# A gated mix of a state-space layer and linear attention: state space in residues modulo 8 instead of 4, with a new list of steps

## The chip, the cores and the metric

The kernel runs on one core of one Trainium2 chip, in one launch. The metric is device time in microseconds, the median of repeated runs. A core has engines with queues of their own: PE (matrix products into PSUM, whose 8 banks hold 512 fp32 per partition each), DVE (vector), ACT (scalar, activation tables), POOL (GpSimd) and SP, which here only issues transfers.

## The reference

One input x of 2048 x 512 (bf16) goes through two branches, and a gate mixes them by rows. Branch A is a diagonal complex state space of 512 states, scanned over 2048 steps; branch B is linear attention with 32 heads of 16, whose feature map is a softmax of a projection and of its negative.

```python
x = A_x
g = sigmoid((x * gate_w).sum(-1, keepdims=True))
# A
dt = exp(log_dt);  Lam_bar = exp(dt * Lam);  B_bar = ((Lam_bar - 1) / Lam)[:, None] * Bmat
Bu = einsum("bld,pd->blp", x, B_bar)
for t in range(L):                      # L = 2048
    h = Lam_bar * h + Bu[:, t];  hs.append(h)
a = 2 * einsum("blp,dp->bld", hs, Cmat).real + x * Dskip
# B
q, k, v = heads(x @ wqkv)               # 32 heads of 16
phi(u) = concat(softmax(u @ w_phi), softmax(-u @ w_phi))
kv = einsum("bhsf,bhsd->bhfd", phi(k), v);  z = phi(k).sum(s)
b = merge((phi(q) @ kv) / (phi(q) @ z + 1e-6)) @ wo
return g * a + (1 - g) * b
```

## The kernel before

All of x, its transposition and all intermediates stay in SBUF. **The order of work on PE, DVE, ACT and SP is written out by hand**: each piece of work is a generator `st_*`, `ORDER` is a list of tokens, and the loop at L807 advances one generator by one step for each token. `k5@2` is the next step of `st_k(5)` with PSUM bank 2, `:D` puts an eviction or a scaling on DVE instead of ACT. Every engine runs its instructions strictly in that order, and waits where an operand or a bank isn't ready.

Rows of x are loaded by residue (L225, L231): `xT` holds the rows with r = 0 modulo 4 first, then r = 1, 2, 3, so that a stretch of 512 columns is one residue over 512 cells.

- Branch B. `st_W` transposes the k weights on PE (L295), `st_B` makes block diagonals BD from Wc (L342), `st_f` and `st_w` fold w_phi into the k and q weights (L427). `st_k`, `st_v`, `st_q` project 128 rows at a time (L467) and evict through `evac` (L123 on ACT, L125 on DVE). `x*`, `n*`, `e*`, `s*` (capitals for q) are the feature map: maximum and minimum trees (L503), differences (L514, L520), exponentials (L142), sums, logarithms. `st_a` collects the sums over keys and the gate in two banks (L570, L574), `st_Y` masks them. `phT` are transpositions of the q features by DMA (L557).
- Branch A. `P`, `P2`, `P3`, `P4`, `M` make the parameters, `M` on POOL; `st_D` the diagonal matrices `dg`; `st_i` the cosine and sine tables T2c, T2s of the scan's rotation (L440 to L450); `st_l` scales B by Lam_bar, and SP transposes it to LBT. With j a block of 128 states, `st_g(j, dst, ri)` forms the inputs: for dst 0 those of residue 1 (with 0 folded in through LBT), for dst 1 those of residue 3, with 2 folded in and, through two matmuls on `dg`, residue 1's. `st_z` rotates, scans 512 cells by `tensor_tensor_scan` with decay r4 (L638), rotates back and writes H3, the state after residue 3. `st_h` makes H1 from H3 with two scalings on ACT (L407) and three sums. `st_c` and `st_r` prepare C and C times Lam_bar, `st_K` the direct matrix K0T.
- Output. `st_y(n)` multiplies 128 rows of states by C (L720, L721) and adds K0T or Dskip (L727, L729); `st_o` divides the attention (L740, L744, L747, L753); `st_O` transposes two of its tiles by DMA to oT (L761); `st_t` adds oT times Wo into st_y's bank (L769) and scales by the gate (L777, L779); `st_R` stores.

The start is fixed by these lines: Wk in one load and the three parameter vectors ahead of Wc on ACT's queue.

```python
nc.scalar.dma_start(out=wk_nat, in_=B_wqkv[:, D:2 * D].rearrange("(k p) n -> p k n", p=P))
for n, src in enumerate((A_Lambda_im, A_Lambda_re, A_log_dt)):
    nc.scalar.dma_start(out=vec_n[4 * n:4 * n + 4, :], in_=src.rearrange("(j p) -> j p", p=P))
nc.scalar.dma_start(out=Wc[:], in_=B_w_phi.rearrange("(k hl) e f -> (hl e) k f", hl=8))
```

Of the kernel before, what the change touches and what calls it, by code (L numbers as in the profile page):

```python
# [34 lines left out]
N0 q11@4 a2 s3 q11 c1 c1 a2 a2 v9@7 e4 s3 a2 q4@4 q4 q5@1 z1 g301@0 c1 c0 X0 N0 e4 q6 q5 X1 N1 s3 z1 z1 z1 Lc g301 X1
g301 g300@4 z0 z0 v11@5 g300 q9 z1 e4 s4 v14@6 g300 g311@0 E0 g311 v14 z1 g311 z0 N1 g310@6 g310 z0 g310 s4 z1 s4
g200@4 v8@1 X1 c3 c3 c3 z1 v9 g311 g201@0 E0 N1 g310 g200 E0 E0 v11 v8 s4 q14@6 z3 g200 g210@7 z3 g201 v15@1 h0 h0
q15@4 s4 S0 h0 v13@5 g201 S0 s4 z3 q14 h0 q15 g210 g210 h0 N1 z3 c2 g211@4 g211 v15 X1 g211 c2 v10@6 z3 z3 v13 c2 S0
r1 c3 r0 g210 S0 S0 s3 v12@5 c2 z3 g211 q13@1 z3 S0 s3 z3 z3 v10 v12 z2 q10@0 y0@4 a3 r1 S0 S0 z2 q13 q12@5 a3 a3 a3
K2@1 q10 h3 h3 h3 q12 K0@0 z2 z2 z2 h3 h3 z2 K2 Lo K3@1 y3@5 r0 K1@6 s4 a4 z2 z2 a4 s4 z2 K0 y1@0 a4 z2 y0 X1 N1 a4 Y  # L40
h1 h1 y3 Y Y Y G K3 S0 y3 K1 h1 h2 r1 y0 h2 h2 h1 h1 h2 h2 END S0 o0@6 r1 E1 E1 o0 o0 y1 S0 o1@2 o1 y1 o0 E1 o1 G G
y4@1 E1 y4 S1 y4 o1 y7@6 S1 G S1 N2 o2@2 r3 r3 o2 o2 S1 S1 o2 y7 r0 y7 S1 y6@7 X2 y6 S1 O0 S1 N2 o3@2 o3 o3 X2 N2 X2
o3 y6 r0 X2 t0 N2 t1 t0 X2 y2@4 N2 t1 X3 y2 r2 r2 S1 y5@0 y5 y5 S1 X3 N3 X3 N3 X3 E2 o4@2 O1 o4 E2 o4 o4 y2 t2 r3 r3
t3 t2 o5@2 N3 t3 y9@4 o5 r2 r2 N3 S1 o5 o5 y13@5 E2 y13 o6@2 y9 E2 o6 X3 y9 N3 R1 o6 E3 o6 o7@2 S2 S2 O2 E3 o7 y13 o7
# [21 lines left out]
def kernel(  # L66
# [60 lines left out]
    NOSYNC = mybir.DependencyInfo(mybir.DependencyClass.NoSync, mybir.DependencyReason.DATA)  # L127
    act_st = {"pre": None, "sins": [], "exps": []}

    def order_after(ins, earlier, why):  # L130
        tc.add_manual_dep(ins.ins, earlier.ins.name, NOSYNC, reason=why)

    def pin_act_set():
        pre = nc.scalar.preload_act_table_set(ACT_SET)
        for s_ in act_st["sins"]:
            order_after(pre, s_, "table set after trig")
        act_st["pre"] = pre
        act_st["sins"] = []
        act_st["exps"] = []

    def aexp(**kw):
        ins = nc.scalar.activation(**kw)  # L142
        order_after(ins, act_st["pre"], "Exp/Ln after table-set preload")
        act_st["exps"].append(ins)
        return ins

    def asin(**kw):
        ins = nc.scalar.activation(func=ACT.Sin, **kw)
        order_after(ins, act_st["pre"], "Sin after preload")
        if not act_st["sins"]:  # L150
            for e_ in act_st["exps"]:
                order_after(ins, e_, "trig batch after the preceding Exp/Ln batch")
        else:
            order_after(ins, act_st["sins"][0], "inside one trig batch")
        act_st["sins"].append(ins)
        return ins

    man_g = tc.manual_schedule(engines={mybir.EngineType.PE, mybir.EngineType.DVE, mybir.EngineType.Activation, mybir.EngineType.SP})
# [10 lines left out]
    nc.scalar.dma_start(out=wk_nat, in_=B_wqkv[:, D:2 * D].rearrange("(k p) n -> p k n", p=P))  # L169
    for n, src in enumerate((A_Lambda_im, A_Lambda_re, A_log_dt)):  # L170
        nc.scalar.dma_start(out=vec_n[4 * n:4 * n + 4, :], in_=src.rearrange("(j p) -> j p", p=P))
    nc.scalar.dma_start(out=Wc[:], in_=B_w_phi.rearrange("(k hl) e f -> (hl e) k f", hl=8))
    pin_act_set()
# [29 lines left out]
    dg = pBC.tile([P, 3, PT, P], BF16, name="dg")  # L203
    DG_NMI, DG_MR, DG_MI = range(3)
    (S_LR, S_LI, S_NMI, S_MR, S_MI, S_NBI, S_BR) = range(7)
    par = pBC.tile([P, 20, PT], F32, name="ssm_par")
    dgs = pBC.tile([P, 7, PT], F32, name="dgs")
    dgv = pBC.tile([P, 3, PT, 4], BF16, name="dgv")
# [169 lines left out]
    def st_M():  # L378
# [12 lines left out]
        nc.gpsimd.tensor_scalar(out=dgs[:, S_NMI, :], in0=dgs[:, S_MI, :], scalar1=-1.0, scalar2=None, op0=ALU.mult)  # L391
        GT(out=r2_, in0=r_, in1=r_, op=ALU.mult)
        GT(out=r4_, in0=r2_, in1=r2_, op=ALU.mult)
        yield

    def st_D():
        nc.vector.tensor_copy(out=dgv[:].rearrange("p k j f -> p (k j) f"),
                              in_=dgs[:, S_NMI:S_NMI + 3].rearrange("p k j -> p (k j)").unsqueeze(2).to_broadcast([P, 3 * PT, 4]))
# [4 lines left out]
        yield
# [444 lines left out]
```

## Time and profile before

| | |
|---|---|
| three runs, median (lowest to highest) | 168.5 us (167.58 to 169.4) |
| profiled execution: time, and the span of its instructions | 168.76 us, 167.0 us |
| busy PE / DVE / ACT / POOL | 154.3 / 142.4 / 127.0 / 7.8 us |
| granted TensorE clock | 0.999 |
| DMA | 16.99 MB, 53846 packets |

A row of the groups reads: line, engine, operation, output <- input by the program's names, shape and count | busy us, mean ns of one | idle time of the engine just before them and what ended it. The mean ns includes an instruction's latency, so a row of instructions that follow each other takes less: two that start 1.04 us apart may show 1.3 us each. The chain goes back from the last instruction to what released each step; its rows give the start in us, the length, engine, tile and line. A row of the timeline merges equal instructions and says in brackets what the engine waited for.

### The profile page before, as it was taken

How to read it: one execution, taken by the hardware profiler on the slowest of the kernel's cores; microseconds unless marked ns; L12 is line 12 of the kernel's file. 1: busy time of each engine (PE TensorE's matmuls, PEld its weight loads, DVE VectorE, ACT ScalarE, POOL GpSimd, SP SyncE). 2: the span in 40 equal slices, each digit the busy share in tenths (PEclk: the TensorE clock that was granted, in tenths of full speed). 3: DMA queues.
4: the chain of work that ended last, by engine and by line, in shares of the span. 5: the costliest groups of instructions: out<-in, count | busy, mean ns of one | idle time of the engine just before them, and what ended most of it. 6: DMA issues, size and time to landing. Idle time of an engine off the chain costs nothing.

```text
span 167.0 us, 2798 instructions
## 1 busy us (share of the span) xinstructions
PE 154.3 (92%) x1022; PEld 75.5 (45%) x1022; DVE 142.4 (85%) x309; ACT 127.0 (76%) x213; POOL 7.8 (5%) x25
## 2 busy tenths in 40 slices
PE   7996999999999999999999999988699997989990
PEld 2642434445554455444444646625354432544540
DVE  4368999999999999999999999999999996635452
ACT  0449999999999999999999987993499781423210
POOL 6014600000000000000000000000000000000000
PEclk9999999999999999999999999999999999999999
DMA  4999910049993018000001360066856569998933
GB/s 133 209 246 293 164 33 0 2 89 204 146 201 56 0 33 96 2 0 0 4 0 23 114 114 4 0 126 56 128 109 152 126 35 177 214 179 216 160 97 126
DMA packets 53846, 16.99 MB, mean 102 GB/s; under 512 B 49224, under 2 KB 53832, under 8 KB 53832
## 3 DMA queue, kind: packets, MB, share of 16 engines
q1 hardware_dynamic: 52688, 16.26, 52.5%
q10 hardware_dynamic: 1080, 0.54, 1.3%
q8 instruction: 8, 0.13, 0.3%
q14 instruction: 6, 0.05, 0.1%
q0 software_dynamic: 64, 0.00, 0.0%
HBM read 2.64 MB, written 2.10 MB: 28 GB/s over the span
## 4 chain that ended last, share of the span: by engine, by line
ACT 50%; PE 24%; DVE 15%; DMA 6%; issue 2%; DVEq 0%
ACT EE L142 11%; ACT Xq L123 9%; PE PS L769 6%; DMA oT<-on 6%; ACT vx L123 4%; ACT uv L123 4%; PE PS L303 4%; PE PS L720 4%; PE PS L721 4%; ACT uv L407 3%; PE PS L727 3%; ACT Wo L407 3%; ACT K0T L407 2%; DVE on L753 2%; DVE sm L503 2%
## 5 line engine op out<-in xcount | busy, mean ns | idle before, releaser
L142 ACT ACTIVATE EE<-EE 128x1024 bf16<-128x1024 bf16 x32 | 36.3, 1198 | 0.8 <-DVE EE L520 0.7
L467 PE MATMUL PS<-WKV,xT 128*128 128x512 bf16 x128 | 29.9, 379 | 2.0 <-ACT WKV L123 1.4
L467 PEld LDWEIGHTS <-xT 128*128 128x128 bf16 x192 | 18.4, 97 | 24.9 <-issue 4.0
L123 ACT CAST Xq<-PS 128x512 bf16<-128x512 f32 x32 | 20.4, 771 | 0.0
L753 DVE TENSOR_TENSOR on<-PS,rd 128x512 bf16<-128x512 f32 x16 | 11.0, 687 | 9.2 <-ACT rd L142 9.1
L769 PE MATMUL PS<-Wo,oT 128*128 128x512 bf16 x64 | 15.1, 379 | 2.2 <-DMA oT<-on 2.2
L587 PE MATMUL PS<-xT,LBT 128*128 128x512 bf16 x64 | 16.3, 379 | 0.0
L584 PE MATMUL PS<-xT,BT 128*128 128x512 bf16 x64 | 16.3, 379 | 0.0
L467 PE MATMUL PS<-Wq,xT 128*128 128x512 bf16 x64 | 15.1, 379 | 0.2 <-ACT Xq L123 0.2
L123 ACT CAST uv<-PS 128x512 bf16<-128x512 f32 x16 | 13.2, 879 | 0.0
L720 PE MATMUL PS<-C,H 128*128 128x512 bf16 x32 | 12.1, 379 | 0.7 <-DVE H L663 0.4
L720 PE MATMUL PS<-WKV,H 128*128 128x512 bf16 x32 | 12.1, 378 | 0.4 <-DVE on L753 0.4
L142 ACT ACTIVATE ld<-PS 128x32 f32<-128x32 f32 x16 | 3.1, 195 | 12.3 <-PE PS L740 11.5
L721 PE MATMUL PS<-C,H 128*128 128x512 bf16 x32 | 12.1, 379 | 0.0
L721 PE MATMUL PS<-WKV,H 128*128 128x512 bf16 x32 | 12.1, 379 | 0.0
L123 ACT CAST vx<-PS 128x512 bf16<-128x512 f32 x16 | 11.6, 824 | 0.0
L407 ACT ACTIVATE CT<-C,dgs 128x1024 bf16<-128x1024 bf16 x8 | 10.0, 1323 | 0.0
L769 PEld LDWEIGHTS <-oT 128*128 128x128 bf16 x64 | 5.9, 98 | 9.0 <-DMA oT<-on 2.8
L503 DVE TENSOR_TENSOR sm<-EE 128x2048 bf16<-128x2048 bf16 (+1 forms) x9 | 9.9, 1099 | 0.0
L514 DVE TENSOR_TENSOR EE<-Xq,mx 128x2048 bf16<-128x2048 bf16 (+1 forms) x9 | 9.9, 1096 | 0.0
L520 DVE TENSOR_TENSOR EE<-mn,Xq 128x2048 bf16<-128x2048 bf16 (+1 forms) x9 | 9.8, 1094 | 0.0
L541 DVE TENSOR_TENSOR EE<-EE,rc 128x2048 bf16<-128x2048 bf16 x8 | 9.6, 1214 | 0.0
(152 smaller groups left out, 303.9 us busy)
## 6 DMA issues: line engine op xcount, KB each, us to landing
out_dram<-ot SPq DMA_DIRECT2D x7, 256.0 KB, 2.6
C<-in_B_wqkv_dram ACTq DMA_DIRECT2D x1, 512.0 KB, 3.9
WKV<-in_B_wqkv_dram SPq DMA_DIRECT2D x1, 512.0 KB, 4.1
Bn<-in_A_B_re_dram SPq DMA_DIRECT2D x1, 512.0 KB
Bn<-in_A_B_im_dram SPq DMA_DIRECT2D x1, 512.0 KB
Wo<-in_B_wo_dram SPq DMA_DIRECT2D x1, 512.0 KB
out_dram<-ot SPq DMA_DIRECT2D x2, 128.0 KB, 1.9
xT<-in_A_x_dram SPq DMA_TRANSPOSE x9, 4.1
```

The lines of the kernel that those rows point to most:

```text
L123: nc.scalar.copy(out=out_ap, in_=in_ap)
L142: ins = nc.scalar.activation(**kw)
L407: nc.scalar.mul(out=out_ap, in_=in_ap, mul=s_)
L467: MM(out=pt[:], lhsT=xT[:, kt, ti * P:(ti + 1) * P], rhs=W[:, kt, :], start=(kt == 0), stop=(kt == KT - 1))
L503: VT(out=dst, in0=cur[:, :, :, 0:n, :], in1=cur[:, :, :, n:2 * n, :], op=op)
L514: VT(out=half(EE, 0), in0=X5, in1=live["mx", p].to_broadcast([P, L, 8, Dh, 4]), op=ALU.subtract)
L584: MM(out=pgq[:], lhsT=BT[:, ri, kt, js], rhs=xT[:, kt, r1 * NC:(r1 + 1) * NC], start=(kt == 0), stop=False)
L587: MM(out=pgq[:], lhsT=LBT[:, ri, kt, js], rhs=xT[:, kt, (r1 - 1) * NC:r1 * NC], start=False, stop=(r1 == 1 and kt == KT - 1))
L720: MM(out=py[:], lhsT=src[:, j, 0, off:off + P], rhs=cw[:, 0, j], start=(j == 0), stop=False)
L721: MM(out=py[:], lhsT=src[:, j, 1, off:off + P], rhs=cw[:, 1, j], start=False, stop=False)
L753: VT(out=live["on", g_][:, u], in0=pn[:, :, :, 0:Dh], in1=rd[:].unsqueeze(3).to_broadcast([P, 2, 16, Dh]), op=ALU.mult)
L769: MM(out=py[:], lhsT=oT[:, g, :], rhs=Wo[:, g, :], start=False, stop=(g == HG - 1))
```

## The change

The state space is cut into residues modulo 8. `xT` holds eight stretches of 256 columns. `st_g` works on two residues at a time in one bank: dst 0 takes residues 1 and 5 (with 0 and 4 folded in), dst 1 residues 3 and 7; the half of residue 3 is evicted to V, and two matmuls of 256 columns on three new diagonals (Lam_bar to the fourth, in `dg` behind the old three) add it to the half of residue 7, which is evicted next. The rotation tables, the rotations and the scan run over 256 cells with decay r8. A new step `st_h4` (tokens `H0` to `H3`) makes the state of residue 3 from that of residue 7, and `st_h` makes those of residues 1 and 5 from both, now with four scalings of 256 cells instead of two of 512.

Wk is loaded in two halves, Wc right behind it on ACT's queue, and the three vectors on GpSimd's queue; the iota goes behind the second identity. POOL's order is now fixed by hand too. Explicit ordering of the activation tables is dropped, since the list sets it. `ORDER` is a new list: Wv (`Lv`) is loaded ahead of x, 12 warm-up steps `Z` are left of 24, v0 and v1 are projected ahead of the first k, Lq goes ahead of the first Lb, Ln ahead of four of the Lx, and the steps between are arranged anew. The diff, cut:

```diff
-Z@0 Z Z Z Z Z Z Z Z W0@1 W1@2 Lx W0:D W1:D W3@3 Lx Lx W2@4 W2:D Lx Z Z Z Z Z Z Z Z Z Z Z Z Z W3 V@1 V B B Lx Lx U P P
...
+Lv Lx Z@0 Z Z Z Z Z Z W0@1 W0:D Z B W1@2 W1 B B W2@3 Z W3@1 B W3 Z Z W2:D V@4 V U P f2@2 f2 Z f1@1 f0@4 U f1 P f3@5 U
+Lx Lx Lx P2 P2 U f0 P2 v0@0 P2 P2 P4 v1@1 P P3 f3 V2@4 P4 k1@2 P4 i0 P2 k0@5 i2 i0 i2 Lx i0 i0 i0 v0 k0 i2 k2@3 P3
...
-    NC = S // 4
+    NC = S // 8
+    N2 = 2 * NC
-    ORD = (3, 1, 0, 2)
+    ORD = (7, 3, 5, 1, 0, 4, 2, 6)
-    nc.scalar.dma_start(out=wk_nat, in_=B_wqkv[:, D:2 * D].rearrange("(k p) n -> p k n", p=P))
+    for h in range(2):
+        nc.scalar.dma_start(out=wk_nat[:, :, 2 * h * P:2 * (h + 1) * P],
+                            in_=B_wqkv[:, D + 2 * h * P:D + 2 * (h + 1) * P].rearrange("(k p) n -> p k n", p=P))
+    nc.scalar.dma_start(out=Wc[:], in_=B_w_phi.rearrange("(k hl) e f -> (hl e) k f", hl=8))
     for n, src in enumerate((A_Lambda_im, A_Lambda_re, A_log_dt)):
-        nc.scalar.dma_start(out=vec_n[4 * n:4 * n + 4, :], in_=src.rearrange("(j p) -> j p", p=P))
-    nc.scalar.dma_start(out=Wc[:], in_=B_w_phi.rearrange("(k hl) e f -> (hl e) k f", hl=8))
+        nc.gpsimd.dma_start(out=vec_n[4 * n:4 * n + 4, :], in_=src.rearrange("(j p) -> j p", p=P))
...
     def st_g(j, dst, ri):
+        def cells(kt, r):
+            return xT[:, kt, :].rearrange("p (r c) -> p r c", r=8)[:, r::4, :]
...
+        evac(V[:, ri, 0:NC], pgq[:, 0:NC])
+        yield
+        MM(out=pgq[:, NC:N2], lhsT=dg[:, da + 3, j, :], rhs=V[:, 0, 0:NC], start=False, stop=False, skip_group_check=True)
+        MM(out=pgq[:, NC:N2], lhsT=dg[:, db + 3, j, :], rhs=V[:, 1, 0:NC], start=False, stop=True, skip_group_check=True)
+        yield
+        evac(V[:, ri, NC:N2], pgq[:, NC:N2])
         yield
...
+    def st_h4(j):
+        sw = pools["sw"][1]
+        prev = H3[:, j, :, ZP - 1:ZP - 1 + NC]
+        mc = sw.tile([P, 2, NC], BF16, name="mc")
+        scaled(mc[:], prev, dgs[:, S_NR, j:j + 1])
+        yield
+        ms = sw.tile([P, 2, NC], BF16, name="ms")
+        scaled(ms[:], prev, dgs[:, S_NI, j:j + 1])
+        yield
+        VT(out=mc[:], in0=mc[:], in1=uv[j][:, 1, :, 0:NC], op=ALU.add)
+        yield
+        VT(out=H3[:, j, 0, ZP + NC:ZP + N2], in0=mc[:, 0, :], in1=ms[:, 1, :], op=ALU.subtract)
+        yield
+        VT(out=H3[:, j, 1, ZP + NC:ZP + N2], in0=mc[:, 1, :], in1=ms[:, 0, :], op=ALU.add)
+        yield
+
     def st_h(j):
...
+        for q, z0 in enumerate((ZP - 1, ZP + NC)):
+            scaled(m5[:, :, q], H3[:, j, :, z0:z0 + NC], dgs[:, S_MR, j:j + 1])
+            yield
+            scaled(n5[:, :, q], H3[:, j, :, z0:z0 + NC], dgs[:, S_MI, j:j + 1])
+            yield
```

More of the change, by code (lines that the diff above doesn't have):

```diff
@@ L35 @@
[L35 to L44, printed above, removed]
@@ new lines @@
+h2 v14@5 s4 v14 H2 h2 a3 H3 H3 h2 q13@7 X1 h3 s4 y2@2 a4 a4 K1@5 q13 q10 h2 K1 a4 H3 N1 E1 a4 E1 K0@0 h2 h2 h3 q15@5
+H3 G S0 X2 H3 Y S0 S0 Y Y y0@1 Y X2 y0 S0 h3 h3 E1 h3 y0 E1 q15 K3@3 X2 h3 N2 K0 y2 h3 END o0@4 y2 K3 S1 S1 o1@6 o0 o0
+o1 G y7@0 y7 o0 r0 S1 X2 S1 o1 S1 o1 N2 o2@4 o2 o2 S1 y1@3 o2 S1 y1 N2 G y7 S1 r1 o3@6 o3 o3 y5@4 N2 X2 y3@5 O0 y3 o3
+N2 G S1 S1 N3 t0 t0:D r1 r1 r0 E2 E2 r0 r1 y1 t1 X3 N3 E2 y5 o4@6 o4 t1 y3 y4@1 r0 N3 N3 X3 O1 t2 E2 t3 o4 o4 S2 y4 t2
+S1 t3 o5@2 o5 o5 X3 o6@6 o5 y6@5 O2 o6 y6 y4 o6 o6 S2 S2 o7@2 r3 o7 X3 y5 y8@6 R0 o7 o7 r3 y9@7 S2 X3 y10@2 S2 r2 S2
@@ L50 @@
+y6 t4 y14@3 t5 O3 t7 t6 N3 S2 S2 S2 r2 r2 r3 r2 r3 y8 S2 S2 t4:D E3 E3 R1 t6:D E3 E3 t5 y14 y14 R2 t7 S3 S3 S3 R3 o8@0
+o8 o8 o9@4 y9 o9 o9 S3 o8 y10 o10@0 S3 S3 o9 O4 y9 S3 o11@4 y10 y8 o10 S3 o10 S3 o10 o11 S3 y13@0 S3 o11 y11@1 t8 o11
+t9 y11 t8 o13@4 t9:D o12@6 o13 O5 y13 y13 o12 o12 o12 o13 o13 o14@6 o14 y11 O6 o15@4 t10 t11 R4 o14 o14 O7 y12@6 y12
+y12 o15 o15 t10 t11 o15 O8 R5 t13 t14 t12 t12:D t13 t14 y15@0 y15 y15 t15 t15:D R6 R7 R8
 """
@@ L125, in evac @@
             nc.vector.tensor_copy(out=out_ap, in_=in_ap)
[L127 to L145, printed above, removed]
-    def asin(**kw):
[L148 to L158, printed above, removed]
+    aexp = nc.scalar.activation
+    def asin(**kw):
+        nc.scalar.activation(func=ACT.Sin, **kw)
+    man_g = tc.manual_schedule(engines={mybir.EngineType.PE, mybir.EngineType.DVE, mybir.EngineType.Activation, mybir.EngineType.SP, mybir.EngineType.Pool})
     man_g.__enter__()
@@ L202 @@
     phT0 = pBC.tile([P, 4, NB, P], BF16, name="phT0")
[L203 to L208, printed above, removed]
+    dg = pBC.tile([P, 6, PT, P], BF16, name="dg")
+    DG_NMI, DG_MR, DG_MI, DG_NNI, DG_NR, DG_NI = range(6)
+    (S_LR, S_LI, S_NMI, S_MR, S_MI, S_NNI, S_NR, S_NI, S_NBI, S_BR) = range(10)
+    par = pBC.tile([P, 21, PT], F32, name="ssm_par")
+    dgs = pBC.tile([P, 10, PT], F32, name="dgs")
+    dgv = pBC.tile([P, 6, PT, 4], BF16, name="dgv")
     Bn = pBC.tile([P, PT, 2, D], BF16, name="Bn")
@@ L221 @@
     T2s = pAC.tile([P, PT, NC], BF16, name="T2s")
-    uv = [pAC.tile([P, 2, 2, NC], BF16, name=f"uv{j}") for j in range(PT)]
+    uv = [pAC.tile([P, 2, 2, N2], BF16, name=f"uv{j}") for j in range(PT)]
     stg_g = tc.tile_pool(name="stage", bufs=2)
     stg = stg_g.__enter__()
-    x_res = x2.rearrange("(c r) d -> r c d", r=4)
+    x_res = x2.rearrange("(c r) d -> r c d", r=8)
     trans = nc.sync.dma_start_transpose
@@ L229, in st_Lx @@
         for t0_, n in XLOADS:
-            c0 = (t0_ % 4) * P
-            trans(out=xT[:, :, t0_ * P:(t0_ + n) * P], in_=x_res[t0_ // 4, c0:c0 + n * P])
+            c0 = (t0_ % 2) * P
+            trans(out=xT[:, :, t0_ * P:(t0_ + n) * P], in_=x_res[t0_ // 2, c0:c0 + n * P])
             yield
@@ L284 @@
     outer = par[:, 6:10, :].rearrange("p (a b) j -> p a b j", a=2)
-    dt_, r_, om_, t0, t1, t2, den_, r2_, r4_, om4 = (par[:, 10 + k, :] for k in range(10))
+    dt_, r_, om_, t0, t1, t2, den_, r2_, r4_, om8, r8_ = (par[:, 10 + k, :] for k in range(11))
     GT = nc.gpsimd.tensor_tensor
     m16 = maskN[:].rearrange("p a b -> p (a b)")
-    order = [4 * g + q for g in ORD for q in range(4)]
+    order = [2 * g + q for g in ORD for q in range(2)]
     live = {}
@@ L366, in st_P4 @@
     def st_P4():
-        VS(out=om4, in0=t0, scalar1=4.0, scalar2=None, op0=ALU.mult)
+        VS(out=om8, in0=t0, scalar1=8.0, scalar2=None, op0=ALU.mult)
         yield
-        VS(out=t2, in0=om4, scalar1=MAGIC, scalar2=MAGIC, op0=ALU.add, op1=ALU.subtract)
+        VS(out=t2, in0=om8, scalar1=MAGIC, scalar2=MAGIC, op0=ALU.add, op1=ALU.subtract)
         yield
-        VT(out=om4, in0=om4, in1=t2, op=ALU.subtract)
+        VT(out=om8, in0=om8, in1=t2, op=ALU.subtract)
         yield
@@ L384, in st_M @@
         GT(out=dgs[:, S_MI, :], in0=outer[:, 0, 1], in1=outer[:, 1, 0], op=ALU.add)
+        mb = dgs[:, S_MR:S_MR + 2, :]
+        GT(out=outer, in0=mb.unsqueeze(2).to_broadcast([P, 2, 2, PT]), in1=mb.unsqueeze(1).to_broadcast([P, 2, 2, PT]), op=ALU.mult)
+        GT(out=dgs[:, S_NR, :], in0=outer[:, 0, 0], in1=outer[:, 1, 1], op=ALU.subtract)
+        GT(out=dgs[:, S_NI, :], in0=outer[:, 0, 1], in1=outer[:, 1, 0], op=ALU.add)
         GT(out=outer, in0=lb.unsqueeze(2).to_broadcast([P, 2, 2, PT]), in1=lam.unsqueeze(1).to_broadcast([P, 2, 2, PT]), op=ALU.mult)
@@ L390, in st_M @@
         GT(out=bb, in0=bb, in1=den_.unsqueeze(1).to_broadcast([P, 2, PT]), op=ALU.mult)
-        nc.gpsimd.tensor_scalar(out=dgs[:, S_NMI, :], in0=dgs[:, S_MI, :], scalar1=-1.0, scalar2=None, op0=ALU.mult)
+        mn3 = dgs[:, S_NMI:S_NMI + 6, :].rearrange("p (a b) j -> p b a j", b=3)
+        nc.gpsimd.tensor_scalar(out=mn3[:, 0], in0=mn3[:, 2], scalar1=-1.0, scalar2=None, op0=ALU.mult)
         GT(out=r2_, in0=r_, in1=r_, op=ALU.mult)
         GT(out=r4_, in0=r2_, in1=r2_, op=ALU.mult)
+        GT(out=r8_, in0=r4_, in1=r4_, op=ALU.mult)
         yield
@@ L439, in st_i @@
         kk_ = tabp.tile([P, NC], F32, name="kk")
-        VS(out=kk_[:], in0=iot[:], scalar1=om4[:, j:j + 1], scalar2=MAGIC, op0=ALU.mult, op1=ALU.add)
+        VS(out=kk_[:], in0=iot[:], scalar1=om8[:, j:j + 1], scalar2=MAGIC, op0=ALU.mult, op1=ALU.add)
         yield
@@ L459, in st_L @@
     def st_L():
-        pin_act_set()
+        nc.scalar.preload_act_table_set(ACT_SET)
         tab_g.__exit__(None, None, None)
@@ L579, in st_g @@
         js = slice(j * P, (j + 1) * P)
[L580 removed]
+        U1, V = uv[j][:, 0], uv[j][:, 1]
+        pgq = bank([P, N2], F32, "pgq")
+        def cells(kt, r):
+            return xT[:, kt, :].rearrange("p (r c) -> p r c", r=8)[:, r::4, :]
         r1 = (1, 3)[dst]
[L582 removed]
         for kt in range(KT):
[L584 removed]
+            MM(out=pgq[:], lhsT=BT[:, ri, kt, js], rhs=cells(kt, r1), start=(kt == 0), stop=False)
         yield
         for kt in range(KT):
[L587 removed]
+            MM(out=pgq[:], lhsT=LBT[:, ri, kt, js], rhs=cells(kt, r1 - 1), start=False, stop=(dst == 0 and kt == KT - 1))
         yield
[L589 to L592 removed]
+        if dst == 0:
+            evac(U1[:, ri, :], pgq[:])
             yield
[L594 removed]
+            return
+        da, db = ((DG_MR, DG_NMI), (DG_MI, DG_MR))[ri]
+        MM(out=pgq[:], lhsT=dg[:, da, j, :], rhs=U1[:, 0, :], start=False, stop=False)
+        MM(out=pgq[:], lhsT=dg[:, db, j, :], rhs=U1[:, 1, :], start=False, stop=True)
+        yield
[5 more added lines that the diff above has]
+        evac(V[:, ri, NC:N2], pgq[:, NC:N2])
         yield
@@ L653, in st_h @@
         U1 = uv[j][:, 0]
-        prev = H3[:, j, :, ZP - 1:ZP - 1 + NC]
-        mc = sw.tile([P, 2, NC], BF16, name="mc")
-        scaled(mc[:], prev, dgs[:, S_MR, j:j + 1])
+        m5 = sw.tile([P, 2, 2, NC], BF16, name="m5")
+        n5 = sw.tile([P, 2, 2, NC], BF16, name="n5", bufs=1)
+        for q, z0 in enumerate((ZP - 1, ZP + NC)):
+            scaled(m5[:, :, q], H3[:, j, :, z0:z0 + NC], dgs[:, S_MR, j:j + 1])
+            yield
+            scaled(n5[:, :, q], H3[:, j, :, z0:z0 + NC], dgs[:, S_MI, j:j + 1])
+            yield
+        mv, nv = (t[:].rearrange("p a q c -> p a (q c)") for t in (m5, n5))
+        VT(out=mv, in0=mv, in1=U1, op=ALU.add)
         yield
-        ms = sw.tile([P, 2, NC], BF16, name="ms")
-        scaled(ms[:], prev, dgs[:, S_MI, j:j + 1])
+        VT(out=H1[:, j, 0, :], in0=mv[:, 0, :], in1=nv[:, 1, :], op=ALU.subtract)
         yield
-        VT(out=mc[:], in0=mc[:], in1=U1, op=ALU.add)
-        yield
-        VT(out=H1[:, j, 0, :], in0=mc[:, 0, :], in1=ms[:, 1, :], op=ALU.subtract)
-        yield
-        VT(out=H1[:, j, 1, :], in0=mc[:, 1, :], in1=ms[:, 0, :], op=ALU.add)
+        VT(out=H1[:, j, 1, :], in0=mv[:, 1, :], in1=nv[:, 0, :], op=ALU.add)
         yield
@@ L783, in st_R @@
         n, L = OGROUPS[g][0], len(OGROUPS[g])
-        r, a = order[n] // 4, order[n] % 4
+        r, a = order[n] // 2, order[n] % 2
         sel["q"].dma_start(out=out_par[:, r, a:a + L, :], in_=live["ot", g][:, 0:L])
@@ L792 @@
         st.update({f"W{j}": st_W(j), f"f{j}": st_f(j), f"w{j}": st_w(j), f"i{j}": st_i(j), f"z{j}": st_z(j), f"r{j}": st_r(j),
-                   f"l{j}": st_l(j), f"c{j}": st_c(j), f"h{j}": st_h(j), f"K{j}": st_K(j)})
+                   f"l{j}": st_l(j), f"c{j}": st_c(j), f"h{j}": st_h(j), f"H{j}": st_h4(j), f"K{j}": st_K(j)})
         for e in range(2):
```

64 lines of the change are left out of this document (28 added, 36 removed).

## The prediction

> **What bounds the kernel now.** I read first the busy time of the engines over five stretches: the start, the long middle, the stretch around the turn to the output phase, the output phase, the end. In the columns, a figure ahead of a bracket is us busy, in the order PE, weight loads, DVE, ACT, POOL.
>
> ```profile
> 0.00:15.00 15.00, 11.83 (x62) 5.73 (x63) 8.31 (x45) 6.04 (x12) 3.75 (x14) 1.00 0.91 203
> 15.00:107.00 92.00, 91.14 (x609) 44.93 (x608) 90.81 (x185) 90.20 (x140) 4.08 (x11) 1.00 0.36 65
> 107.00:135.00 28.00, 24.64 (x177) 12.18 (x177) 27.13 (x57) 21.38 (x39) 0.00 (x0) 1.00 0.60 104
> 135.00:163.10 28.10, 26.72 (x176) 12.67 (x175) 15.41 (x24) 9.35 (x25) 0.00 (x0) 1.00 0.92 161
> 163.10:167.00 3.90, 0.00 (x0) 0.00 (x0) 0.75 (x1) 0.00 (x0) 0.00 (x0) 0.97 0.39 133
> ```
>
> From 15 to 107 us three engines are full together; from 107 to 135 only DVE is; afterwards PE. The busy time of a matmul holds its drain, so I count PE by the distance between starts instead: 0.216 us for 512 columns (eight take 1.90 in the chain below, the last 0.38 with its drain), in the timeline 0.056 for 128 columns, 0.106 for a transpose, 0.033 for 68, 0.025 for one. 616 x 0.216 + 256 x 0.033 + 68 x 0.056 + 16 x 0.106 + 64 x 0.025 and two small ones: 148.6 us. The last matmul ends at 163.1, so PE stood 14.3 us. Running the same count along the timeline puts 6.2 of it before 15 us, 1.6 from 15 to 107, 4.8 from 107 to 135, 1.7 after. **PE's own work is the bound; what can be won is these 14.3 us.**
>
> Next the start of the timeline:
>
> ```profile
> 0.79 0.42 ACTq L169 DMA_DIRECT2D C<-in_B_wqkv_dram  x1
> 5.45 0.42 ACTq L172 DMA_DIRECT2D Wc<-in_B_w_phi_dram  x1
> 9.79 0.49 DVE L342 TENSOR_TENSOR BD<-Wc,mask 128x128 bf16<-128x128 bf16 x2
> 13.84 10.54 PE L467 MATMUL PS<-WKV,xT 128*128 128x512 bf16 x45 [1.35 <-ACT WKV L123]
> ```
>
> and of the waits in total:
>
> ```profile
> ACT L134 <- DMA xT<-in_A_x_dram: 5.9, 1, 5.9
> PE PS L769 <- DMA oT<-on: 2.2, 2, 1.3
> PE PS L740 <- DVE on L753: 1.8, 4, 0.9
> ```
>
> Wc was issued only at 5.45, when the first xT transposition had landed: eight DMA semaphores go round, three of them taken by vec_n ahead of Wc. BD, the folds and all k projections hang on Wc, so PE's dense stream starts at 13.84, after 24 warm-up matmuls.
>
> Last the chain that ended last:
>
> ```profile
> 24.72 2.42 ACT Xq L123 x5
> 94.20 1.06 ACT mc L407
> 113.24 5.07 DMA oT<-on
> 118.36 1.90 PE PS L769 x8
> 134.21 0.68 DVE on L753
> ```
>
> From 24 to 95 us it is ACT without a break; then DVE; then oT transpositions (5 us each) and PE.
>
> **The change, engine by engine.** Durations, from the groups with forms apart (count, us, mean ns):
>
> ```profile
> L638 DVE TENSOR_TENSOR_SCAN w<-ssm_par,mc 128x512 bf16<-128x512 f32 x8 | 9.5, 1211 | 0.0
> L407 ACT ACTIVATE mc<-H,dgs 128x1024 bf16<-128x1024 bf16 x4 | 5.4, 1353 | 1.6 <-DVE w L638 0.8 <-DVE H L648 0.7
> L503 DVE TENSOR_TENSOR mn<-Xq 128x1024 bf16<-128x1024 bf16 x7 | 4.8, 684 | 0.2 <-ACT Xq L123 0.2
> L503 DVE TENSOR_TENSOR mn<-mn 128x512 bf16<-128x512 bf16 x7 | 2.9, 416 | 0.0
> L503 DVE TENSOR_TENSOR mx<-mx 128x256 bf16<-128x256 bf16 x9 | 2.5, 280 | 0.0
> ```
>
> DVE: halving 1024 to 512 saves 0.27, 512 to 256 saves 0.135. Sixteen rotations halve from 1024 (-4.3), eight sums of st_z from 512 (-1.1), eight scans fall from 1.13 between starts to about 0.60 (-4.2), the tables of st_i lose 0.53 per j (-2.1). st_h4 adds per j one add over 512 and two over 256 (+3.0, part of it st_z's own H3 writes getting shorter: net +1.9), dg doubles (+0.8), two st_l scalings move here (+0.8), one output scaling leaves (-0.7). Sum -8.8: 137.8 to 129.0.
>
> ACT: 1024 elements with a scale from dgs take 1.05 between starts (35.34 to 37.43 in the chain for two); by the slope of EE (0.95 at 1024) against T2s (0.52 at 512), 512 takes 0.615. Eight such become 24: +6.4. Eight 512-column uv evictions (0.48) become 16 of 256 (0.26): +0.4. Sin tables -1.9, st_l -2.1, one output scaling +0.6. Sum +3.4: 120.5 to 123.9. Not shown are 256-column evictions and 2x256 scalings; each is bounded below by half of its double (0.24, 0.52) and above by the whole double (0.48, 1.05), 40 instructions, so ACT's sum is at least 2.6 less or at most 14 more than I take; I stay by the slope, since rows of four sizes lie on one line.
>
> PE: 12 warm-ups go (-2.6), 16 matmuls of 256 columns come (0.109 each, between the 128 and 512 rows, +1.7): 147.7.
>
> POOL: three vec_n loads (0.77 and 0.53 us for its vec_m loads) ahead of make_identity make ident and identf about 1.9 later (identf 3.0 to 4.9), hidden behind Wk's landing at 4.7; without that cover W0 starts up to 0.5 later. Eight more tiny GpSimd operations in st_M (0.2 to 0.7 each) take under 3 us and run beside the k projections; dg, for which they are needed, is moved behind s1 in the list.
>
> SP and DMA: Wv goes ahead of all xT tiles (one more 0.58 issue, 0.5 MB), Bn ahead of the last four xT transpositions. By the before rates (about 240 GB/s in the first 20 us) 2.0 MB have to land before k6's tile: 11 us, and PE asks for it near 12.6. In Wc's place four slots are now free, so nothing makes Wc wait: it lies behind Wk on ACT's queue and lands about 6. Lq's two transpositions now go ahead of the first BT on SP (1.3 us of issue each): BT0 is issued near 18 (19.02 before) and PE asks for it at sum 24.8, clock about 28. The iota, moved behind identf on POOL, is done by 5.5, and st_i reads it near 9.5. At these covers the moves cost nothing; a tile that is late costs PE its lateness once.
>
> **The start.** Both Wk halves share the engines with Wv, so the second lands near 6 (1 MB at the rate above from 2 us). W3's eviction 7.3, folds 7.3 to 8, four WKV evictions until 9.8; v0 and v1, which need no fold, fill PE from 8. k1 starts near 10 without a gap, where before it was 13.84. ACT's lag (clock less the sum of its work so far) is 10.5 before, when the tables are back at 22.7 with 12.2 us of work done, and 10.8 at 94.2 with 83.4 done: nothing was lost between. In the new list ACT's first eight evictions, two exps and the sine tables follow each other from W1 on, lag 6.3; I take **7.0**, with 5.5 and 10.5 (as before) as ends.
>
> **Middle and output phase.** I add the sums along both step lists and look for the tightest consumer:
>
> | step | before PE / ACT / DVE | after |
> |---|---|---|
> | tables set back (L) | 14.0 / 12.2 / 12.9 | 16.6 / 12.3 / 12.2 |
> | END | 99.0 / 93.1 / 99.7 | 97.0 / 95.1 / 93.1 |
> | whole | 148.6 / 120.5 / 137.8 | 147.7 / 123.9 / 129.1 |
>
> Before, PE's tightest ACT step is y0 taking the bank of g211 (PE 83.4, ACT 80.2): PE's lag must be ACT's less 3.2, that is 7.6 at 94 us with ACT at 10.8, as counted. Then y10 takes o7's bank with DVE's sum 0.7 ahead of PE's: with DVE's lag at 12 that gives 12.5, as counted at 135. The on-to-t steps leave only 3.4 to 5.6 for a 5.07 us transfer, hence the waits for oT. After, the tightest ACT step is o0 on q15's bank (97.0 and 94.7: less 2.4); DVE is never nearer than 4.0 behind PE; the on-to-t steps leave 7.7 or more. So PE's lag after o0 is 7.0 - 2.4 + 0.3 (calibrated on before) = 4.9. DVE waits for ACT in the new h steps (up to 2.7), ACT for DVE at E2, PE for ACT at t3: +1.0. For transfers late in the end, which no view can show, 0 to 1.7 (as before after 135): +1.5.
>
> The sum: 147.7 + 4.9 + 1.0 + 1.5 = 155.1 for the last matmul; + 3.9 for scaling and store, whose steps are the same: **span 159.0**; + 1.8 that the profiled execution has around its span (168.76 less 167.0) = 160.8. That execution is 0.3 over the median of the runs, 168.5, so **160.6**. By the ends: 157.6 (lag 5.5, no late transfer); 164 (lag 10.5).
>
> **The rivals.**
> Vectors late: loads that POOL issues could be held back by DVE. For it: vec_m, issued at 1.93 from POOL, took until 5.96. Against it: DVE does little then. Were the descriptors written only when DVE's head work ends (mask16, 4.06), vec_n would land 4.0 later, near 8.1 instead of 5.6: the first exp, which stands ahead of three WKV evictions on ACT, holds k back by 2.5: 163. The Trainium skill's page "SBUF — State Buffer", section "Who interferes with whom", says that descriptors for a DMA issued from GpSimd cannot be written while DVE runs a two-port copy or scaling, which speaks against this move. No row of before shows such a stall.
>
> Start hidden: Wk, Wv and xT together land no earlier, ACT's lag stays 10.5: 164.
>
> Late stalls stay: oT transfers collide with phT and output stores as before (6.5 us of PE instead of 2.5): 164.6. Against it is the spacing in the list.
>
> ACT decides, slower: the 40 new short ACT instructions cost nearly as much as their doubles. ACT then reaches END 11 to 13 us later, PE waits for evictions (o0 takes q15's bank at once), and the output phase, 51 us of PE, starts so much later: 171. From about 0.2 us above my price of each it eats the whole gain. Against it: EE, sines and Ln scale with size; for it: ACT has no slack before END.
>
> No change at all: the start hidden and the late stalls kept, 168.
>
> **How the numbers follow.** Forecast 0.58, late vectors 0.08, start hidden 0.13, late stalls 0.10, no change 0.04, ACT decides 0.07. About 1% is what a measurement of this kernel can tell from no change; the first four are more than that below 168.5: faster 0.88, same 0.05, slower 0.07. The range, 157 to 166.5, leaves out the last two and the unlikeliest good end.
>
> **What would show it.** Right: Wc issued near 2; dense PE from 8 to 10, 12 warm-ups; evictions of 256 columns 0.26 apart, scans 0.6; DVE near 133 busy, ACT 130; no DVE "on" wait on PE; last matmul near 155. Wrong: PE gaps behind uv evictions or H from 40 to 100, k after 12, or "oT" waits over 2 us.

## The result and the profile after

The changed kernel takes **161.5 us** (median of 4 runs, 161.15 to 161.73) where the kernel before, run beside it, took 168.3: ratio 0.959, 95% interval 0.953 to 0.965. The forecast was 160.6. The profiled execution took 161.66 us, its span 159.9.

The busy times over the same five stretches as before (PE, weight loads, DVE, ACT, POOL; the last two stretches end with this kernel's last matmul and span):

```profile
0.00:15.00 15.00, 12.66 (x66) 6.26 (x67) 8.72 (x47) 7.78 (x15) 4.85 (x15) 1.00 0.91 225
15.00:107.00 92.00, 91.68 (x637) 46.26 (x636) 90.95 (x214) 91.81 (x164) 5.69 (x17) 1.00 0.38 67
107.00:135.00 28.00, 26.57 (x196) 13.49 (x195) 26.50 (x52) 23.23 (x42) 0.00 (x0) 1.00 0.79 142
135.00:156.30 21.30, 21.27 (x137) 10.16 (x133) 6.74 (x11) 6.44 (x17) 0.00 (x0) 1.00 0.77 155
156.30:159.90 3.60, 0.00 (x0) 0.00 (x0) 0.75 (x1) 0.00 (x0) 0.00 (x0) 1.00 0.11 37
```

From 15 to 107 us PE, DVE and ACT are full, as before. From 107 on PE is nearly full. Counted as in the prediction, PE has 147.8 us of work (148.6 before) and stands 8.4 us (14.3 before): 5.5 before 15 us (6.2), 1.1 to 107 (1.6), 1.7 to 135 (4.8), nothing after (1.7).

The start, from the timeline:

```profile
0.79 1.10 ACTq L145 DMA_DIRECT2D C<-in_B_wqkv_dram  x2
0.80 0.45 SPq L233 DMA_DIRECT2D WKV<-in_B_wqkv_dram  x1
1.92 0.53 ACTq L147 DMA_DIRECT2D Wc<-in_B_w_phi_dram  x1
7.90 0.90 DVE L319 TENSOR_TENSOR BD<-Wc,mask 128x128 bf16<-128x128 bf16 x4 [1.33 <-DMA Wc<-in_B_w_phi_dram]
10.68 1.89 PE L450 MATMUL PS<-WKV,xT 128*128 128x512 bf16 x8
20.01 1.28 ACT L443 ACT_TABLE_LOAD   x1
```

Wc is issued at 1.92 instead of 5.45, but BD still waits for it until 7.90. The dense stream starts at 10.68 with v0; the forecast had 8 to 10. The last line is the third and last table load on ACT, before which both kernels have given ACT 12.2 to 12.3 us of work; it started at 21.42 before. It serves below as the mark of how late the start is.

The waits for a late operand, and the transpositions in the chain that ended last:

```profile
PEld L752 <- DMA phT<-EE: 2.4, 2, 1.6
PE PS L752 <- DMA phT<-EE: 1.4, 2, 1.1
DVE BD L319 <- DMA Wc<-in_B_w_phi_dram: 1.3, 1, 1.3
PEld L781 <- DMA oT<-on: 0.3, 1, 0.3
```

```profile
22.87 1.90 ACT EE L509 x2
109.54 5.00 DMA phT<-EE
126.19 6.24 DMA phT<-EE
```

PE's waits for "on" are gone and the one for oT is down to 0.3 (2.8 in weight loads before). New are two waits of PE for phT, ended at 114.6 and 132.5 us, which hold it 0.5 and 1.3 (before, only weight loads waited for phT, 0.7 in all).

The new forms, from the groups with forms apart (the mean holds the wait of a pipelined instruction for the one ahead, so the distance between starts in the timeline is the price: 0.252 for the eviction of 256 columns, 0.60 for the scan, 0.61 for the scalings):

```profile
L124 ACT CAST uv<-PS 128x256 bf16<-128x256 f32 x16 | 8.4, 615 | 0.0
L633 DVE TENSOR_TENSOR_SCAN w<-ssm_par,mc 128x256 bf16<-128x256 f32 x8 | 5.2, 682 | 0.0
L390 ACT ACTIVATE m<-H,dgs 128x512 bf16<-128x512 bf16 x8 | 8.7, 1091 | 0.0
```

### The profile page after: what moved, and what is told of

Same layout as the page of the kernel before. It is cut to its first block, busy times and chain, and to the rows that moved or that the text cites. A ratio compares the mean times of both kernels' runs of the same rounds, so it can differ in the third digit from the quotient of the medians.

```text
span 159.9 us, 2853 instructions
## 1 busy us (share of the span) xinstructions
PE 152.2 (95%) x1026; PEld 76.2 (48%) x1026; DVE 133.7 (84%) x322; ACT 129.3 (81%) x236; POOL 10.5 (7%) x32
## 4 chain that ended last, share of the span: by engine, by line
ACT 47%; PE 29%; DMA 13%; SPq 6%; issue 2%; DVE 0%; DVEq 0%
ACT EE L509 11%; ACT Xq L124 8%; DMA phT<-EE 7%; PE PS L732 6%; PE PS L733 6%; PE PS L781 6%; ACT vx L124 5%; ACT uv L124 4%; PE PS L739 4%; DMA C<-in_B_wqkv_dram 3%; PE PS L752 3%; ACT m L390 3%; DMA CT<-in_A_C_im_dram 3%; ACT n L390 3%; SPq L218 3%; SPq L229 2%
## 5 line engine op out<-in xcount | busy, mean ns | idle before, releaser
L509 ACT ACTIVATE EE<-EE 128x1024 bf16<-128x1024 bf16 x32 | 35.2, 1230 | 0.6 <-DVE EE L503 0.6
L450 PE MATMUL PS<-WKV,xT 128*128 128x512 bf16 x128 | 29.4, 379 | 0.0
L124 ACT CAST Xq<-PS 128x512 bf16<-128x512 f32 x31 | 21.7, 766 | 0.0
L450 PE MATMUL PS<-Wq,xT 128*128 128x512 bf16 x64 | 16.1, 379 | 0.0
L791 DVE TENSOR_SCALAR ot<-PS,G 128x512 bf16<-128x512 f32 x6 | 4.5, 749 | 12.4 <-PE PS L781 12.3
L124 ACT CAST uv<-PS 128x256 bf16<-128x256 f32 (+1 forms) x24 | 14.1, 676 | 0.0
L789 ACT ACTIVATE ot<-PS,G 128x512 bf16<-128x512 f32 x10 | 6.7, 682 | 7.2 <-PE PS L781 7.2
L124 ACT CAST vx<-PS 128x512 bf16<-128x512 f32 x16 | 12.5, 825 | 0.0
L732 PEld LDWEIGHTS <-H 128*128 128x128 bf16 x64 | 6.3, 98 | 6.6
```

The source lines that it names most:

```text
L124: nc.scalar.copy(out=out_ap, in_=in_ap)
L450: MM(out=pt[:], lhsT=xT[:, kt, ti * P:(ti + 1) * P], rhs=W[:, kt, :], start=(kt == 0), stop=(kt == KT - 1))
L509: aexp(out=EE[:, l_], in_=EE[:, l_], func=ACT.Exp)
L732: MM(out=py[:], lhsT=src[:, j, 0, off:off + P], rhs=cw[:, 0, j], start=(j == 0), stop=False)
```

## The experiments

The theory: the gain is PE's idle time, won by an earlier start, by a DVE that is 9 us lighter, and by a step list that no longer asks for oT as soon as it is issued. Rivals: the start alone, the lighter DVE alone, the list alone. The table puts all runs side by side; "last matmul" and "table load" (ACT's third) are from the profiled execution, and their difference is what the kernel needs once its start is over. Each ratio is to the kernel before in the same session (medians 168.0 to 168.3).

| kernel | median us | ratio to before (95%) | table load | last matmul | difference |
|---|---|---|---|---|---|
| before | 168.3 | 1 | 21.42 | 163.09 | 141.67 |
| before, lighter DVE | 166.99 | 0.994 (0.991 to 0.997) | 20.74 | 160.78 | 140.04 |
| before, new start | 165.33 | 0.984 (0.977 to 0.991) | 19.08 | 159.94 | 140.86 |
| before, both | 163.98 | 0.976 (0.969 to 0.982) | 19.14 | 158.52 | 139.38 |
| after | 161.5 | 0.959 (0.953 to 0.965) | 20.01 | 156.27 | 136.26 |
| after, lighter DVE | 161.57 | 0.961 (0.958 to 0.964) | 19.68 | 155.61 | 135.93 |
| after, DVE loaded | 174.9 | 1.040 (1.033 to 1.046) | 19.88 | 169.10 | 149.22 |
| after, ACT loaded | 167.75 | 0.998 (0.995 to 1.001) | 19.84 | 162.49 | 142.65 |
| after, vec_n on ACT's queue | 164.09 | 0.976 (0.971 to 0.980) | 20.86 | 157.08 | 136.22 |
| after, Wk in one load | 160.94 | 0.958 (0.953 to 0.963) | 18.61 | 154.81 | 136.20 |
| after, Wv later | 159.66 | 0.951 (0.948 to 0.955) | 17.92 | 153.88 | 135.96 |
| the same, two y steps moved | 159.32 | 0.948 (0.940 to 0.955) | 18.32 | 153.73 | 135.41 |
| the same, Wc first | 159.8 | 0.952 (0.948 to 0.957) | 17.95 | 153.38 | 135.43 |
| y steps moved, Wk in one load | 158.73 | 0.943 (0.940 to 0.946) | 17.96 | 153.35 | 135.39 |

Kernels whose start is the same differ in the table load by up to 0.7 us from one profile to the next (21.42 and 20.74 in the first two rows, 19.68 to 20.01 in four of the others), so smaller differences in that column say nothing by themselves.

**DVE loaded.**

```
 VT(out=mc[:], in0=V, in1=c2, op=ALU.mult)
+VT(out=mc[:], in0=V, in1=c2, op=ALU.mult)
...  (so with ms, with the scan, and with mc and ms after it)
```

> The changed kernel, with the four rotations and both scans of st_z issued twice each (the same values written again, no step of the list moved): 16 x 0.335 + 8 x 0.60 = 10.2 us more DVE work, all of it before the turn to the output phase. If the 6 us of PE idle that the change took away went because DVE became lighter, DVE is again the late engine at the turn: the list leaves DVE 4.0 us of room behind PE, so PE stands some 6 us more, 167 to 168. If they went because the new list keeps on, oT and t farther apart, whatever DVE carries, the added work is taken up: 161.5 to 163.

It took 174.9, more than either. The timeline shows why the load was more than 10.2:

```profile
61.99 0.41 DVE L621 TENSOR_TENSOR mc<-uv,T2c 128x512 bf16<-128x512 bf16 x1
62.44 0.43 DVE L622 TENSOR_TENSOR mc<-uv,T2c 128x512 bf16<-128x512 bf16 x1
62.78 0.42 DVE L625 TENSOR_TENSOR ms<-uv,T2s 128x512 bf16<-128x512 bf16 x1
```

A repetition into the same tile starts 0.45 after the first, not 0.34, because the program makes it wait for the end of the first; a repeated scan adds 0.71. So 16 x 0.45 + 8 x 0.71 = 12.9 us were added, and the difference column grew by 13.0. In the long middle DVE alone is full now, and PE waits for it in the a steps, and elsewhere for ACT, which waits for DVE in its turn:

```profile
15.00:107.00 92.00, 80.26 (x508) 39.23 (x515) 91.06 (x211) 81.18 (x143) 5.69 (x17) 0.98 0.31 55
PEld L553 <- DVE EE L524: 7.0, 4, 3.8
```

The list keeps no room of 4.0 us for DVE, and "the list alone" falls: with DVE busy for 146.0 us, 3.6 more than in the kernel before, the new list takes 6.9 us more than the old one. With the two lists at the same DVE work nothing was run; at 1 us of time for each us added, putting back the 8.7 us that DVE lost would take the changed kernel to some 170 us (an estimate from these two runs), still above the old list.

**Lighter DVE in the kernel before.**

```
-VT(out=mc[:], in0=V, in1=c2, op=ALU.mult)
... (ms, and the two sums, likewise)
-nc.vector.tensor_tensor_scan(..., data1=mc[:, ri, :], ...)
+nc.vector.tensor_tensor_scan(..., data1=V[:, ri, :], ...)
```

> The kernel before, with the first rotation of st_z left out (the scan reads V as it is, so the state is another one): 8 products over 1024 columns at 0.605 and 8 sums over 512 at 0.335, 7.5 us less DVE work, list and start unchanged. If a lighter DVE alone takes away the late idle time, the 4.8 us of PE idle between 107 and 135 shrink to what ACT's lag leaves, 163.5 to 164.5. If it needs the new list (on to t too close for a 5 us transposition), at most 1 to 2 us are won, 166.5 to 167.5.

166.99, the second: 7.5 us less DVE work buys 1.0 us in the median, 1.6 in the difference column. "The lighter DVE alone" falls too.

**The start in the kernel before, alone and with the lighter DVE.**

```
-W2:D Lx Z Z Z Z Z Z Z Z Z Z Z Z Z W3
+W2:D Lx Z W3
...
+for h in range(2): nc.scalar.dma_start(out=wk_nat[..half h..], ...)
-    nc.scalar.dma_start(out=vec_n[4 * n:4 * n + 4, :], ...)
+    nc.gpsimd.dma_start(out=vec_n[4 * n:4 * n + 4, :], ...)
```

> The kernel before, with the start of the change alone: the three vec_n loads on GpSimd's queue, Wk in halves, and 12 of the 13 warm-up matmuls after W2 taken out of the list. Wc's issue is then no longer held back by vec_n. If the start is most of the gain, because ACT, DVE and PE are all full from 15 to 107 us and every us by which they start earlier is kept: BD near 6.5 where it was 9.79, the dense stream near 10.7 where it was 13.84, and 164.5 to 165.5. If the late waits (on, oT, phT) take back what the start gives, 166.5 to 167.5.

> The same, and also without the first rotation of st_z, 7.5 us of DVE work, as in the earlier run of the kernel before. If start and lighter DVE are all that the change brings, the two together give what the changed kernel has, 161 to 162.5. If the rest of the step list (the order of y, o, O and t, the banks) is needed to use them, 1 to 2 us below the start alone, 163.5 to 166.

165.33, the first, and 163.98, the second. BD starts at 7.44 (6.5 expected) and the dense stream at 11.50, so the table load is 2.3 us earlier and the time 2.8 shorter: the start is kept. With the lighter DVE, 1.35 more. The rest, 2.5 us to 161.5, needs what is left of the change, the state split itself and the rest of the list. (This start is the better one: the table load of the changed kernel came only 1.4 earlier than before, not 2.3, so the rest is worth more than 2.5 by itself: 3.1 in the difference column.) What is still lost in the old list, with both, are its late waits, these and one of 0.9 for an ACT scaling of C:

```profile
PE PS L736 <- DVE on L749: 1.1, 3, 0.5
PEld L765 <- DMA oT<-on: 0.8, 2, 0.4
PEld L736 <- DMA phT<-EE: 0.7, 2, 0.5
PE PS L765 <- DMA oT<-on: 0.5, 1, 0.5
```

PE stands 4.3 us after 107 in that run (gaps of the length of one matmul missing from the trace not counted), against 1.7 in the changed kernel. By the sums along the lists, the new one has also given PE 14.0 us of useful work before the table load, the old 8.8 (warm-ups left out). So the difference column compares these two lists only roughly, and which of the two, the state split or the list, makes how much of the 2.5 us was not tried alone.

**ACT loaded.**

```
 evac(V[:, ri, 0:NC], pgq[:, 0:NC])
+evac(V[:, ri, 0:NC], pgq[:, 0:NC])
... (the other half likewise)
```

> The changed kernel, with each of the 16 uv evictions of 256 columns issued twice: 16 x 0.252 = 4.0 us more on ACT, all of it before END, no step of the list moved. If ACT has no room before END (PE's lag is ACT's less 2.4), 165 to 166. If ACT had room, as DVE was said to have, 161.5 to 163.

167.75, past the first. ACT's busy time grew by 5.8 us (135.1 against 129.3) and the difference column by 6.4, 0.40 for each repetition: a repeated eviction, which waits for the end of the first, starts 0.41 after it (median of the 16), not 0.25. ACT has no room at all:

```profile
15.00:107.00 92.00, 86.44 (x573) 42.59 (x581) 85.58 (x202) 91.47 (x168) 5.69 (x17) 1.00 0.35 59
```

ACT alone is full there now; PE and DVE wait for it.

**Lighter DVE in the changed kernel.** The same edit as in the kernel before.

> The changed kernel with the first rotation of st_z left out (the scan reads V as it is, so the state is another one): 8 products at 0.335 and 8 sums at 0.202, 4.3 us less DVE work. If DVE alone sets the pace from 15 to 107, as one could read from its 10.2 us of added work costing 13, 157 to 158.5. If DVE is only even with ACT and PE, and all three are full, ACT holds the place and at most 0.5 us are won: 161 to 161.6.

161.57, no gain: the second. Adding to DVE costs in full, taking from it gives nothing: DVE is level with ACT, not ahead of it. DVE's work can no longer be cut with profit by itself; a lighter ACT was not tried.

**vec_n back on ACT's queue.**

```
-nc.gpsimd.dma_start(out=vec_n[4 * n:4 * n + 4, :], ...)
+nc.scalar.dma_start(out=vec_n[4 * n:4 * n + 4, :], ...)
... (and Wc's load behind them)
```

> The changed kernel, with the three vec_n loads back on ACT's queue, between Wk and Wc, as before. If POOL's queue made vec_n late, it lands near 5, the first exp runs 1 to 2 us earlier, but Wc is issued later: 160.5 to 161.5. If the order on ACT's queue and its round of semaphores is what counts, Wc is issued only when an earlier load has landed, near 5.5, lands near 9, and BD, the folds and k1 come 1 us later: 162 to 163.

164.09, just past the second. ACT's queue stops again, here before the third vec_n, which takes over the semaphore of Wk's first half and is issued when that has landed:

```profile
2.61 0.27 ACTq L148 DMA_DIRECT2D vec_n<-in_A_Lambda_re_dram  x1
5.51 0.25 ACTq L148 DMA_DIRECT2D vec_n<-in_A_log_dt_dram  x1
5.80 0.40 ACTq L149 DMA_DIRECT2D Wc<-in_B_w_phi_dram  x1
9.17 0.90 DVE L319 TENSOR_TENSOR BD<-Wc,mask 128x128 bf16<-128x128 bf16 x4 [2.57 <-DMA Wc<-in_B_w_phi_dram]
```

With vec_n on GpSimd's queue the medians are 2.6 us lower. The profiled execution is the quickest of its four, 162.86; there the table load is 0.85 later and the difference column unchanged. What made the other three 1.2 to 1.5 us longer than this one, no profile shows.

**Wv later.**

```
-Lv Lx Z@0 Z ...
+Lx Z@0 Z ...
...
-Lx Lx Lx P2 P2 ...
+Lx Lv Lx Lx P2 P2 ...
```

> The changed kernel, with Wv's load moved from the head of SP's queue to behind the second xT transposition. If the first 8 us are bound by the bytes that the engines move and Wv stands in the way of Wk, Wc, vec_n and xT0, these land 1 to 2 us earlier (Wc near 6, vec_n near 6.5), the dense stream begins near 9 and ACT's lag of 9.0 falls by as much: 159.8 to 160.5. If they are late for another reason (the queue they are on, a fixed time per small load), they land as now and v0 waits for Wv: 161.5 to 162.5.

159.66, the first, and 0.1 below its range. Nothing but 0.5 MB was moved out of the way, and all that stood behind it came earlier: Wk's first half landed at 3.73 (5.46), xT0 at 5.74 (7.79), Wc at 6.14 (7.80), the last vec_n at 6.34 (8.04).

```profile
6.24 0.90 DVE L319 TENSOR_TENSOR BD<-Wc,mask 128x128 bf16<-128x128 bf16 x4 [0.68 <-DMA Wc<-in_B_w_phi_dram]
8.53 1.89 PE L450 MATMUL PS<-WKV,xT 128*128 128x512 bf16 x7
17.92 1.28 ACT L443 ACT_TABLE_LOAD   x1
```

The table load is 2.1 us earlier and the last matmul 2.4. Wv at the head of SP's queue is a part of the change that costs.

**Two y steps moved into the gaps**, on top of that.

```
-E2 y5 o4@6 o4 t1 y3 y4@1 ...
+E2 y5 y3 o4@6 o4 t1 y4@1 ...
...
-... S3 S3 S3 R3 o8@0 o8 o8 o9@4 y9 o9
+... S3 S3 S3 R3 y9 o8@0 o8 o8 o9@4 o9
```

> The changed kernel with Wv's load behind the second xT transposition, as in the run before, and two steps of y (1.7 us of PE work each, their operands long ready) moved ahead of the o4 and o8 that wait 0.5 and 1.3 us for phT. If these two waits are paid for in full by the last matmul, 159.66 less 1.3 to 1.7: 157.9 to 158.4. If later steps (on, oT, the stores) give them back, 159.2 to 159.8.

159.32: by the median the second. The difference column fell from 136.0 to 135.4, and so it is in the two other kernels with this edit: of the 0.3 in front of o4 0.1 is left, and the 1.1 in front of o8 became 0.4 there and 0.4 in front of o10. That second wait is not for phT: o10 takes o8's bank and now waits until DVE is done with it (`on`), because the y step that stood between them was the one moved ahead. So 0.6 is won after the start, less than half of the two waits, and the profiled start happened to be 0.4 later.

**Wc first** (its load ahead of the two Wk halves), on top of that.

> The changed kernel with Wv's load behind the second xT transposition and the two steps of y moved, as in the run before, and Wc's load (16 KB) issued ahead of the two Wk halves. If the loads of the first microseconds land in the order in which they are issued, Wc lands near 3.5 where it was 6.1, BD no longer stands between W1 and W2's eviction on DVE, and folds and dense stream come 0.5 to 1 us earlier: 158.3 to 158.9. If vec_n (6.3) or Wk's second half (5.3) hold the folds just as long, 159.1 to 159.6.

159.8, no gain in the median, and past the second: three of six executions at 158.8 to 159.0, just below the four without this edit (159.1 to 159.5), three at 160.6 to 161.0, which one profile cannot explain. In the profiled one, of 158.76, Wc landed at 3.06, but Wk's halves at 5.18 and 6.04 (3.96 and 5.53 with Wk first); W0 starts at 5.23, BD at 6.00, the dense stream at 8.55.

**Wk in one load**, in the changed kernel and with Wv later and the y steps moved.

```
-for h in range(2): nc.scalar.dma_start(out=wk_nat[..half h..], ...)
+nc.scalar.dma_start(out=wk_nat, in_=B_wqkv[:, D:2 * D]...)
```

> The changed kernel with Wk in one load. W0 then starts when all of Wk has landed, near 6.4 where it was 5.5. If Wc and vec_n, landed at 7.8 and 8.0, are what the folds wait for, W0 to W3 are still done in time and nothing changes: 161.2 to 161.8. If the transpositions and their evictions decide, 162.2 to 162.6.

> The kernel with Wv later and the two steps of y moved (159.32), with Wk in one load instead of halves. In the run with Wk in one load and all else as changed, Wc landed at 6.39 where it was 7.80. If the halves delay Wc here too, it lands near 5.5, the folds start 0.5 earlier and the time is 158.3 to 158.9. If W0, which waits for all of Wk (near 4.9, halves 3.7 and 5.3), takes this back, 159.2 to 159.8.

160.94 and 158.73, in both cases about 0.6 below the halves, with intervals that overlap. The halves brought nothing that can be measured: W0 starts 0.6 later without them (6.09), but Wc is issued 0.6 earlier, landed 1.4 earlier, and BD started at 6.87. The last kernel is the fastest here, 0.943 of the kernel before.

## Why the prediction was right, and where it was off

The direction, the engine sums and most of the places held. Its sum was 0.9 us short in the profiled execution (160.8 against 161.66), and term by term:

- **PE's work**, 147.7: measured 147.8. DVE busy 133.7 (133 forecast), ACT 129.3 (130). The prices by the slope held: 0.252 for 0.26, 0.61 for 0.615, 0.60 for 0.60. With them "ACT decides" fell away; that ACT had no room, which it was built on, is true (ACT loaded).
- **ACT's lag**, taken as 7.0: mis-sized. The tables were back at 21.3 with 12.3 us of work done, so 9.0. The step that failed is "at these covers the moves cost nothing": Wv was costed at zero because PE asks for k6's tile late, and Wc was said to land near 6 because nothing held its issue. But of the loads issued within the first 3 us Wv landed at 5.19, Wk at 5.46 and 6.41, and only behind this 1 MB xT0 at 7.79, Wc at 7.80 and the last vec_n at 8.04: the smallest were among the last. With Wv moved the tables are back at 19.2, a lag of 6.9. (The rate used there, "about 240 GB/s in the first 20 us", is that of the second 10 us, 242; the first 10 had 183. It did no harm: Wk's second half landed at 6.41 where 1 MB at 240 from 2 us gives 6.4.)
- **PE's lag after o0**, 4.9 = 7.0 - 2.4 + 0.3: measured 6.6, which is 9.0 - 2.4 (6.9 with the 0.3). The tie was right, the lag put into it was not. The difference column, 136.0 to 136.3 in the changed kernel and the three that alter its start alone, says the same: after the table load every us of start is a us of time.
- **Circle of h steps and late transfers**, 1.0 + 1.5: measured 1.8 (0.5 and 1.3, both phT). The waits for "on" and oT went as forecast.
- **Tail**, 3.9: measured 3.6; around the span 1.76 for 1.8.

So -0.7 (late waits) and -0.3 (tail) hid part of +1.7 (start), and +0.1 came with PE's work.

One step was wrong without showing in the number: "DVE is never nearer than 4.0 behind PE". The sums left out that DVE starts late and waits too. In the timeline PE waits 0.2 us at 38.1 for the product that completes EE, and the last but one of these products ends at 92.31 where PE's a step starts at 93.07: 0.8 us of room, not 4.0, and DVE loaded found none. That the 8.7 us taken from DVE were used up by the new list, not left over, was missed.

Of the rivals, "vectors late" had the right symptom, vec_n at 8.04 (8.1), and the wrong cause. With Wv moved, vec_n lands 0.9 to 1.7 us earlier although DVE's and GpSimd's work up to 5 us starts at the same times to 0.01 us; what moved is the bytes in flight. The Trainium skill ("Trainium Kernel Development and Optimization", section "Key Constraints") says that DMAs from SP's, ACT's and GpSimd's queues run on the same 16 engines, and that issuing from several saves only issue time. The runs agree as far as they go: with vec_n on GpSimd's queue Wc is issued 3.9 us earlier (1.92 for 5.80) but lands only 1.3 us earlier (7.80 for 9.07). "Start hidden" came in part: of 3.5 us of ACT's lag that were to be won, 1.5 were.

## What to carry to other kernels

Where several engines are full together, compare the lists by one mark that all variants pass, such as a table load: what comes before it and what comes after it then add up, and most edits here show in one of the two. Lists that do different work before the mark can't be compared so. A large load that nobody needs soon is not free at the start of a kernel: it delays the smallest load that everything hangs on, so order by the first consumer, and cost bytes issued in the same microseconds together. Work taken from one engine, here DVE, won 1.0 to 1.35 us in the old list and, taken out once more, nothing in the new one, where that engine is as tight as the others.

## What was not expected of the hardware

- Loads of 1 KB on GpSimd's queue took 5.1 to 5.5 us to land with Wk, Wv and xT0 in flight, and 3.8 to 4.2 with Wv issued later.
- A DVE product of 512 columns that rewrites the tile of the one ahead starts 0.45 us after it, one into another tile 0.34; for scans of 256 columns it is 0.70 to 0.72 against 0.60, and for ACT evictions of 256 columns 0.39 to 0.44 (once 0.53) against 0.25. In each pair the program makes the second wait for a semaphore that the first raises at its end, and it starts 0.03 us after that end; without the wait, products and scans start 0.08 us before the end of the one ahead.
- A load of 256 KB issued 0.46 us later, behind one of 16 KB, landed 1.2 us later (5.18 for 3.96); how much of that is the order and how much differs from one execution to the next was not measured.
